# Decode attention with a SwiGLU block: two V rows per matmul, an identity held over twelve matmuls, one broadcast of the row maxima, and the last weight in three loads

## The chip, the cores and the metric

One core of a Trainium2 chip runs the kernel. The metric is the device time of one execution in microseconds (us), the median over several runs. "The changed kernel" is the kernel after the change; "before" is the one it was made from. A profile is one execution taken by the hardware profiler, and its times count from the start of the span. The profile counts 16 DMA engines for the core's loads; I call them queue engines. In the listings PE is the engine of the matmuls, PEld its loading of weights, DVE and ACT the engines of the elementwise work, and POOL an engine that is idle here after the first microseconds. A semaphore is a counter that engines wait for; PSUM is the memory that matmuls write to.

## The reference, cut to what matters

```python
# B=4 sequences, one new token each, D=640; 32 heads, 4096 cached keys, head size 192; F=1536
q = (layernorm(x) @ wq)                                  # per head: [192]
scores = einsum("bhqd,bhkd->bhqk", q, k_cache) * 192**-0.5
o = einsum("bhqk,bhkd->bhqd", softmax(scores), v_cache)
h = x + o.reshape(4, 1, 32*192) @ wo
out = h + (silu(ln(h) @ w_gate) * (ln(h) @ w_up)) @ w_down
```

K and V are 201 MB each in bf16 and every byte is used once. Everything else is small.

## The kernel before

The kernel goes through 64 steps. Step i treats two heads of one sequence: one K load and one V load of 3 MB each, into a ring of six buffers. A load is issued when the buffer's last reader is done.

```python
def tt(i, h):       # DVE: K times q, half a buffer at a time; 128 calls in all
    ... tensor_tensor(out=prod, in0=ring[K][half], in1=q broadcast, op=mult)

def red(i, h):      # PE: sum over the head size, 12 matmuls with the same identity as weights
    for j in range(J):
        ... e.matmul(psR[n % 3][:, 0:512], lhsT=identH, rhs=prod[..., j*R:(j+1)*R],
                     start=(j == 0), stop=(j == J - 1))

def max_b(i):       # PE: the two heads' maxima, each broadcast to 64 partitions
    for hh in range(2):
        ... e.matmul(psS[64*hh:64*hh+64, 128:129], lhsT=ones_row, rhs=negMc[0:1, hh:hh+1], ...)

def pv(i, ...):     # PE: 64 V rows per partition, one row per matmul, four column groups in turn
    for t in range(lo, hi):
        n = t % 4
        ... e.matmul(psO[p % 2][32*n:32*n+8, 0:192], lhsT=pbuf[b][:, t, :], rhs=v[:, t, :], ...)
```

After each group of four steps the sums are copied out of PSUM (`evac`), transposed by small fp32 matmuls (`o_t`), scaled (`o_tc`, giving `OT`) and multiplied by `wo`. At the end come the second layer norm (`lnT`), the gate and up products, their transpose `guT`, and 48 matmuls with `w_down`. The three last weights are loaded behind K and V into freed ring buffers:

```python
wg_land = dma("sp", ... wgsb, S_ring[...], [behind(n0)])
wu_land = dma("sp", ... wusb, S_ring[...], [behind(n0 + 1)])
wd_land = dma("sp", ... wdsb, S_ring[...], [behind(n0 + 2)])     # one load, 1920 KB
```

## Time and profile before

| | before |
|---|---|
| median of the first 3 runs | 1005.88 us (1005.46 to 1006.93) |
| instructions on PE (matmuls and weight loads) | 13472 |
| DMA in the loop | 425 to 435 GB/s by slice, mean 429, every slice full |
| instruction packets of 16 KB | 53 |
| last load: first and last of its 16 landings | 988.5 and 999.9 us |

The slices of the page before divide the span in 40. `DMA` is the busy share of the 16 queue engines in tenths.

```profile
PE   0676666666576576576576676676676676576585
DMA  9999999999999999999999999999999999999995
GB/s 394 426 435 430 426 431 427 428 431 427 429 429 427 429 429 431 428 427 431 427 430 428 430 426 431 425 433 430 425 431 429 428 429 428 431 428 429 428 425 248
```

DMA is full in every slice but the last, while PE has idle time throughout. So the loop is paced by the loads, at a mean of 429 GB/s, and computing less should not speed it up.

The page's DMA queues (packets, MB, share of the 16 engines' time) and its groups of instructions (line, engine, operation, shapes, count | busy us, mean ns | idle before, and what ended it):

```profile
q1 hardware_dynamic: 21472, 424.29, 98.9%
q8 instruction: 53, 0.87, 0.4%
...
L309 DVE TENSOR_TENSOR prod<-ring,qb 128x6144 f16<-128x6144 bf16 x128 | 429.2, 3354 | 308.3 <-DMA ring<-in_A_k_cache_dram 301.2
L319 PE MATMUL pb<-prod,identH 128*128 128x512 f16 x1536 | 470.6, 472 | 3.2 <-DVE prod L309 3.2
L319 PEld LDWEIGHTS pb<-prod,identH 128*128 128x128 f16 x1536 | 167.8, 116 | 262.1 <-issue 168.9
...
L381 PE MATMUL pb<-ring,pbuf 128*8 128x192 bf16 x4096 | 95.8, 246 | 0.2 <-ACT pbuf L356 0.2
L381 PEld LDWEIGHTS pb<-ring,pbuf 128*8 128x8 bf16 x4096 | 81.3, 87 | 3.7 <-issue 0.4
```

DVE waits 301 us for K. `q8 instruction`: the core also fetches its own program, here in 53 packets of 16384 bytes that take 1.07 us each in the mean.

The table of windows before (window, its length, then busy us and count of PE, PEld, DVE, ACT, POOL; granted clock as a share of PE's full clock, DMA share, GB/s):

```profile
300.00:305.00 5.00, 0.00 (x0) 0.00 (x0) 3.66 (x2) 0.00 (x0) 0.00 (x0) 0.76 1.00 428
985.00:990.00 5.00, 4.14 (x151) 3.42 (x146) 0.47 (x3) 3.15 (x8) 0.00 (x0) 1.00 0.87 371
990.00:995.00 5.00, 1.97 (x34) 0.84 (x26) 2.56 (x10) 1.58 (x2) 0.00 (x0) 0.70 0.55 231
995.00:1000.00 5.00, 2.15 (x28) 0.51 (x20) 1.40 (x2) 0.49 (x1) 0.00 (x0) 0.50 0.34 144
```

The last load was issued at 976.3, yet from 988 on only half of the queue engines, and later fewer, still work (DMA share 0.55 from 990, 0.34 from 995). The trace records 16 landings on the semaphore of each of these loads. I read them as one from each of the 16 queue engines. Sorted, for an early load and for the last one (wd), before:

```
a K load at the start   28.2 28.2 28.2 28.3 28.4 28.4 28.5 28.5 | 28.6 28.7 28.7 28.7 28.7 28.8 28.8 29.2
wd, the last load      988.5 988.7 988.8 988.9 989.2 990.1 991.9 993.0 | 998.1 998.4 998.4 999.0 999.3 999.6 999.7 999.9
```

Early, all 16 engines agree within 1.0 us. At the end eight are done by 993.0 and eight come at 998.1 to 999.9, so that first and last are 11.4 us apart. The distance grows evenly: in loads that begin to land at 162, 431, 698 and 966 us the last landing is 2.7, 5.3, 8.4 and 11.3 us behind the first. The kernel's wait for a load ends with the last landing, for wd at 999.9.

The tail of the timeline before (start, duration, instruction, count, idle before and what ended it):

```profile
995.39 1.77 PE L502 MATMUL pb<-wu_sb,lnT 128*4 128x384 bf16 x20
...
997.87 0.85 DVE L508 STREAM_TRANSPOSE guT<-gu 128x384 bf16<-128x384 bf16 x1
...
1000.05 1.77 PE L512 MATMUL pb<-wd_sb,guT 128*4 128x160 bf16 x48 [2.90 <-DMA wd_sb<-in_B_w_down_dram]
1001.87 0.32 DVE L515 CAST outsb<-pb 128x160 bf16<-128x160 f32 x1 [3.16 <-PE pb L512]
```

`guT` is ready at 998.7, but the matmuls with `w_down` wait for the last landing of wd at 999.9 and start at 1000.05.

### The profile page before, as it was taken

How to read it: one execution, taken by the hardware profiler on the slowest of the kernel's cores; microseconds unless marked ns; L12 is line 12 of the kernel's file. 1: busy time of each engine (PE TensorE's matmuls, PEld its weight loads, DVE VectorE, ACT ScalarE, POOL GpSimd, SP SyncE). 2: the span in 40 equal slices, each digit the busy share in tenths (PEclk: the TensorE clock that was granted, in tenths of full speed). 3: DMA queues.
4: the chain of work that ended last, by engine and by line, in shares of the span. 5: the costliest groups of instructions: out<-in, count | busy, mean ns of one | idle time of the engine just before them, and what ended most of it. 6: DMA issues, size and time to landing. Idle time of an engine off the chain costs nothing.

```text
span 1004.3 us, 14803 instructions
## 1 busy us (share of the span) xinstructions
PE 645.7 (64%) x6736; PEld 296.7 (30%) x6736; DVE 547.5 (55%) x450; ACT 119.7 (12%) x412; POOL 4.5 (0%) x19
## 2 busy tenths in 40 slices
PE   0676666666576576576576676676676676576585
PEld 0232232333232232232232232232332332232243
DVE  2546546546546546546546546546546546546562
ACT  0111011011011011011010110110111010111012
POOL 1000000000000000000000000000000000000000
PEclk9787887887887888887887887887887877877887
DMA  9999999999999999999999999999999999999995
GB/s 394 426 435 430 426 431 427 428 431 427 429 429 427 429 429 431 428 427 431 427 430 428 430 426 431 425 433 430 425 431 429 428 429 428 431 428 429 428 425 248
DMA packets 21582, 425.24 MB, mean 423 GB/s; under 512 B 2448, under 2 KB 2448, under 8 KB 4496
## 3 DMA queue, kind: packets, MB, share of 16 engines
q1 hardware_dynamic: 21472, 424.29, 98.9%
q8 instruction: 53, 0.87, 0.4%
q14 instruction: 9, 0.07, 0.0%
q10 hardware_dynamic: 48, 0.01, 0.0%
HBM read 424.29 MB, written 0.01 MB: 422 GB/s over the span
## 4 chain that ended last, share of the span: by engine, by line
DMA 68%; PE 21%; DVE 10%; SPq 1%; issue 0%; ACTq 0%; ACT 0%
DMA ring<-in_A_k_cache_dram 64%; PE pb L319 15%; DVE prod L309 7%; PE pb L381 3%; DMA wd_sb<-in_B_w_down_dram 2%; DMA xrow<-in_A_x_dram 2%; DVE sc L325 1%; PE pb L334 1%; SPq L294 1%; PE pb L276 1%; DVE msb L330 0%; PE pb L344 0%; PE pb L365 0%; PE pb L398 0%; SPq L300 0%
## 5 line engine op out<-in xcount | busy, mean ns | idle before, releaser
L309 DVE TENSOR_TENSOR prod<-ring,qb 128x6144 f16<-128x6144 bf16 x128 | 429.2, 3354 | 308.3 <-DMA ring<-in_A_k_cache_dram 301.2
L319 PE MATMUL pb<-prod,identH 128*128 128x512 f16 x1536 | 470.6, 472 | 3.2 <-DVE prod L309 3.2
L319 PEld LDWEIGHTS pb<-prod,identH 128*128 128x128 f16 x1536 | 167.8, 116 | 262.1 <-issue 168.9
L334 PE MATMUL pb<-identF,msb 128*1 128x128 f32 x128 | 34.7, 369 | 320.5 <-DVE msb L330 320.5
L325 DVE TENSOR_REDUCE sc<-pb 128x32 f32<-128x512 f32 x128 | 88.0, 688 | 111.8 <-PE pb L319 111.8
L334 PEld LDWEIGHTS pb<-identF,msb 128*1 128x1 f32 x128 | 5.5, 80 | 335.9 <-DVE msb L330 335.9
L349 ACT ACTIVATE negM<-pb 128x1 f32<-128x1 f32 x64 | 11.0, 171 | 721.0 <-PE pb L344 721.0
L381 PE MATMUL pb<-ring,pbuf 128*8 128x192 bf16 x4096 | 95.8, 246 | 0.2 <-ACT pbuf L356 0.2
L381 PEld LDWEIGHTS pb<-ring,pbuf 128*8 128x8 bf16 x4096 | 81.3, 87 | 3.7 <-issue 0.4
L356 ACT ACTIVATE pbuf<-sc,negM 64x64 bf16<-64x64 f32 x128 | 73.7, 576 | 3.1
L356 ACT ACTIVATION_READ_ACCUMULATOR pbuf<-sc,negM 64x1 f32 x128 | 41.6, 325 | 0.0
L371 ACT ACTIVATE qb<-pb 128x192 bf16<-128x192 f32 x64 | 21.1, 330 | 102.5 <-PE pb L365 102.5
L344 PEld LDWEIGHTS pb<-negMc,ones_row 1*64 1x64 f32 x256 | 12.8, 136 | 35.0 <-issue 33.4
L344 PE MATMUL pb<-negMc,ones_row 1*64 1x1 f32 x256 | 18.3, 206 | 0.7 <-DVE negMc L338 0.7
L365 PE MATMUL pb<-qsb,sel 4*64 4x192 bf16 x128 | 17.2, 265 | 1.0 <-ACT qsb L280 0.6
L338 DVE TENSOR_REDUCE negMc<-pb 1x2 f32<-1x128 f32 x64 | 17.4, 271 | 0.5 <-PE pb L334 0.5
L246 PE MATMUL pb<-mv,quadm 128*128 128x2 f32 x4 | 1.0, 312 | 23.4 <-DVE mv L244 23.4
L330 DVE TENSOR_REDUCE msb<-sc 128x1 f32<-128x64 f32 x64 | 14.1, 220 | 2.2
L365 PEld LDWEIGHTS pb<-qsb,sel 4*64 4x64 bf16 x128 | 6.7, 101 | 27.9 <-issue 26.3
L398 PE MATMUL pb<-r,orow 128*64 128x4 f32 x192 | 11.1, 233 | 0.4 <-ACT orow L387 0.4
L398 PEld LDWEIGHTS pb<-r,orow 128*64 128x64 f32 x192 | 9.7, 173 | 2.1 <-ACT orow L387 0.7
L242 DVE BATCH_NORM_STATS2 stats<-xrow 128x6 f32<-128x160 bf16 x1 | 0.3, 328 | 16.2 <-DMA xrow<-in_A_x_dram 16.2
(60 smaller groups left out, 71.8 us busy)
## 6 DMA issues: line engine op xcount, KB each, us to landing
ring<-in_A_k_cache_dram SPq DMA_DIRECT2D x64, 3072.0 KB, 30.4
ring<-in_A_v_cache_dram SPq DMA_DIRECT2D x63, 3072.0 KB, 23.4
wq_sb<-in_A_wq_dram SPq DMA_DIRECT2D x1, 7680.0 KB, 21.2
wo<-in_A_wo_dram SPq DMA_DIRECT2D x16, 480.0 KB, 23.8
ring<-in_A_v_cache_dram SPq DMA_DIRECT2D x2, 1536.0 KB, 19.7
wg_sb<-in_B_w_gate_dram SPq DMA_DIRECT2D x1, 1920.0 KB, 26.2
wu_sb<-in_B_w_up_dram SPq DMA_DIRECT2D x1, 1920.0 KB, 19.4
wd_sb<-in_B_w_down_dram SPq DMA_DIRECT2D x1, 1920.0 KB, 23.6
```

The source lines that it names most:

```text
L309: tk["tt", n] = op("dve", lambda e: e.tensor_tensor(out=prod[n % NPR][:, :, :], in0=ring[slot[c]][:, h * TH:(h + 1) * TH, :], in1=qbs[i % ...
L319: tk["red", n] = op("pe", lambda e, j=j: e.matmul(psR[n % 3][:, 0:TH * R], lhsT=identH[:, :], rhs=prod[n % NPR][:, :, j * R:(j + 1) * R], ...
L325: tk["rsum", n] = op("dve", lambda e: e.tensor_reduce(sc[i % 3][:, h * TH:(h + 1) * TH], psR[n % 3][:, 0:TH * R].rearrange("q (t r) -> q t ...
L330: tk["rmax", i] = op("dve", lambda e: e.tensor_reduce(msb[i % 2][:, 0:1], sc[i % 3][:, :], AX.X, ALU.max), [g("rsum", 2 * i), g("rsum", 2 ...
L334: tk["maxT", i] = op("pe", lambda e: e.matmul(psS[0:1, 0:128], lhsT=msb[i % 2][:, 0:1], rhs=identF[:, :], start=True, stop=True), [g("rmax ...
L338: tk["hmax", i] = op("dve", lambda e: e.tensor_reduce(negMc[i % 2][0:1, 0:2], psS[0:1, 0:128].rearrange("o (h q) -> o h q", h=2), AX.X, AL ...
L344: tk["maxB", i] = op("pe", lambda e, hh=hh: e.matmul(psS[64 * hh:64 * hh + 64, 128:129], lhsT=ones_row[0:1, :], rhs=negMc[i % 2][0:1, hh:h ...
L356: tk["exp", i] = op("act", lambda e, hh=hh, r=r: e.activation(out=pbuf[b][r, :, 2 * b + hh], in_=sc[i % 3][r, :], func=ACTF.Exp, bias=negM ...
L365: tk["qb", i] = op("pe", lambda e, hh=hh: e.matmul(psQ[64 * hh:64 * hh + 64, 0:DH], lhsT=sel[32 * n:32 * n + B, b, :], rhs=qsb[32 * n:32 * ...
L371: tk["qbc", i] = op("act", lambda e: e.activation(out=qbs[i % 2][:, :], in_=psQ[:, 0:DH], func=ACTF.Copy, scale=QS), [g("qb", i), g("tt", ...
L381: tk["pv", i] = op("pe", lambda e, t=t, n=n: e.matmul(psO[p % 2][32 * n:32 * n + 2 * B, 0:DH], lhsT=pbuf[b][:, t, :], rhs=v[:, t, :], star ...
L398: tk["oT", p] = op("pe", lambda e, j=j, hh=hh: e.matmul(psO[p % 2][64 * hh:64 * hh + 64, 256 + 4 * j:260 + 4 * j], lhsT=orow[p % 2][:, j:: ...
```

## The change

The intent is less work for PE, and a shorter wait for the last weight. PV takes two V rows per matmul: 16 columns of weights against 384 columns, of which only the two diagonal blocks are of use; the blocks that mix rows are left alone in PSUM. The identity is loaded for the first of 12 matmuls and kept for the other 11. The two maxima are broadcast by one matmul. wd comes in three loads.

```diff
+def held_matmul(e, out, lhsT, rhs, start, stop):
+    return e.add_instruction(mybir.InstMatmult(... ldweights=False, ...))
...
     def red(i, h):
-            tk["red", n] = op("pe", lambda e, j=j: e.matmul(
+            tk["red", n] = op("pe", lambda e, j=j: (e.matmul if j == 0 else partial(held_matmul, e))(
...
     def max_b(i):
-        for hh in range(2):
-            ... psS[64 * hh:64 * hh + 64, 128:129], lhsT=ones_row, rhs=negMc[i % 2][0:1, hh:hh + 1]
+        ... psS[:, 128:130], lhsT=ones_row, rhs=negMc[i % 2][0:1, 0:2]
...
     def pv(i, lo=0, hi=T):
-        for t in range(lo, hi):
-            n = t % 4
+        for t in range(lo, hi, 2):
+            n = (t // 2) % 4
-                psO[p % 2][32 * n:32 * n + 2 * B, 0:DH], lhsT=pbuf[b][:, t, :], rhs=v[:, t, :],
+                psO[p % 2][32 * n:32 * n + 4 * B, 0:2 * DH],
+                lhsT=pbuf[b][:, t:t + 2, :].rearrange("q t m -> q (t m)"),
+                rhs=v[:, t:t + 2, :].rearrange("q t d -> q (t d)"),
...
     def o_t(p):                     # sums the two diagonal blocks: twice the transposes
+                for k in range(2):
+                    ... lhsT=orow[p % 2][:, k * DH + j:(k + 1) * DH:3], start=(k == 0), stop=(k == 1)
...
-    wd_land = dma("sp", ... wdsb, S_ring[(n0 + 2) % NS], [behind(n0 + 2)])
+    WDC = [(0, 6, sem("s_wd0")), (6, 10, sem("s_wd1")), (10, CF, sem("s_wd2"))]
+    for lo, hi, k in WDC:
+        t = dma("sp", ... wdsb[:, lo:hi, :], k, [behind(n0 + 2)])     # 960, 640 and 320 KB
```

More of the change, by code (lines that the diff above doesn't have):

```diff
@@ L1 @@
 import math
+from functools import partial
 import concourse.bass as bass
@@ L91, in emit @@
         block.sync(run("sp"))
+def held_matmul(e, out, lhsT, rhs, start, stop):
+    return e.add_instruction(mybir.InstMatmult(
+        name=e.bass.get_next_instruction_name(), engine=mybir.EngineType.PE, start_tensor_calc=start,
+        stop_tensor_calc=stop, tile_size=(128, 128), tile_position=(0, 0), ldweights=False,
+        ins=[e.lower_ap(rhs), e.lower_ap(lhsT, for_matmul_weights=True)], outs=[e.lower_ap(out)]))
 class ExitGuard:
@@ L118, in build_kernel @@
     NS, NPR = 6, 3
+    OC = 2 * DH
     QS = 2.0 ** -4
@@ L145, in build_kernel @@
     r32 = sb("r32", [128, 32], FP32)
-    ones_row = sb("ones_row", [1, 64], FP32)
+    ones_row = sb("ones_row", [1, 128], FP32)
     epsv = sb("epsv", [128, 1], FP32)
@@ L155, in build_kernel @@
     negMc = [sb(f"negMc{j}", [1, 2], FP32) for j in range(2)]
-    negM = [sb(f"negM{j}", [128, 1], FP32) for j in range(2)]
+    negM = [sb(f"negM{j}", [128, 2], FP32) for j in range(2)]
     lsb = [sb(f"lsb{j}", [128, B], FP32) for j in range(2)]
     invL = sb("invL", [128, B], FP32)
-    orow = [sb(f"orow{j}", [128, DH], FP32) for j in range(2)]
+    orow = [sb(f"orow{j}", [128, 2 * DH], FP32) for j in range(2)]
     OT = [sb(f"OT{j}", [128, 3, B], BF16) for j in range(2)]
@@ L342, in max_b @@
     def max_b(i):
-        for hh in range(2):
-            tk["maxB", i] = op("pe", lambda e, hh=hh: e.matmul(
-                psS[64 * hh:64 * hh + 64, 128:129], lhsT=ones_row[0:1, :], rhs=negMc[i % 2][0:1, hh:hh + 1],
-                start=True, stop=True), [g("hmax", i), pool_done])
+        tk["maxB", i] = op("pe", lambda e: e.matmul(
+            psS[:, 128:130], lhsT=ones_row[0:1, :], rhs=negMc[i % 2][0:1, 0:2],
+            start=True, stop=True), [g("hmax", i), pool_done])
     def neg_m(i):
-        tk["negM", i] = op("act", lambda e: e.activation(out=negM[i % 2][:, :], in_=psS[:, 128:129], func=ACTF.Copy,
+        tk["negM", i] = op("act", lambda e: e.activation(out=negM[i % 2][:, :], in_=psS[:, 128:130], func=ACTF.Copy,
                                                          scale=alpha), [g("maxB", i)])
@@ L356, in exps @@
             tk["exp", i] = op("act", lambda e, hh=hh, r=r: e.activation(
-                out=pbuf[b][r, :, 2 * b + hh], in_=sc[i % 3][r, :], func=ACTF.Exp, bias=negM[i % 2][r, 0:1],
+                out=pbuf[b][r, :, 2 * b + hh], in_=sc[i % 3][r, :], func=ACTF.Exp, bias=negM[i % 2][r, hh:hh + 1],
                 scale=alpha, accum_out=lsb[p % 2][r, b:b + 1]),
@@ L377, in pv @@
         v = ring[slot[c]]
-        for t in range(lo, hi):
-            n = t % 4
+        for t in range(lo, hi, 2):
+            n = (t // 2) % 4
             land = landed[c][min(t // TH, len(landed[c]) - 1)]
             tk["pv", i] = op("pe", lambda e, t=t, n=n: e.matmul(
-                psO[p % 2][32 * n:32 * n + 2 * B, 0:DH], lhsT=pbuf[b][:, t, :], rhs=v[:, t, :],
-                start=(b == 0 and t < 4), stop=(b == B - 1 and t >= T - 4)), [land, g("exp", i), g("otc", p - 2)])
+                psO[p % 2][32 * n:32 * n + 4 * B, 0:2 * DH],
+                lhsT=pbuf[b][:, t:t + 2, :].rearrange("q t m -> q (t m)"),
+                rhs=v[:, t:t + 2, :].rearrange("q t d -> q (t d)"),
+                start=(b == 0 and t < 8), stop=(b == B - 1 and t >= T - 8)), [land, g("exp", i), g("otc", p - 2)])
         released[c] = tk["pv", i]
     def evac(p):
-        tk["evac", p] = op("act", lambda e: e.activation(out=orow[p % 2][:, :], in_=psO[p % 2][:, 0:DH],
+        tk["evac", p] = op("act", lambda e: e.activation(out=orow[p % 2][:, :], in_=psO[p % 2][:, 0:2 * DH],
                                                          func=ACTF.Copy), [g("pv", B * p + B - 1), g("oT", p - 2)])
@@ L397, in o_t @@
             for hh in range(2):
-                tk["oT", p] = op("pe", lambda e, j=j, hh=hh: e.matmul(
-                    psO[p % 2][64 * hh:64 * hh + 64, 256 + 4 * j:260 + 4 * j], lhsT=orow[p % 2][:, j::3],
-                    rhs=r32[:, hh:2 * B:2], start=True, stop=True), [g("evac", p), pool_done])
+                for k in range(2):
+                    tk["oT", p] = op("pe", lambda e, j=j, hh=hh, k=k: e.matmul(
+                        psO[p % 2][64 * hh:64 * hh + 64, OC + B * j:OC + B * (j + 1)],
+                        lhsT=orow[p % 2][:, k * DH + j:(k + 1) * DH:3],
+                        rhs=r32[:, 2 * B * k + hh:2 * B * (k + 1):2], start=(k == 0), stop=(k == 1)),
+                        [g("evac", p), pool_done])
     def inv_l(p):
@@ L406, in o_tc @@
         tk["otc", p] = op("dve", lambda e: e.tensor_tensor(
-            out=OT[p % 2][:, :, :], in0=psO[p % 2][:, 256:256 + 3 * B].rearrange("q (j b) -> q j b", b=B),
+            out=OT[p % 2][:, :, :], in0=psO[p % 2][:, OC:OC + 3 * B].rearrange("q (j b) -> q j b", b=B),
             in1=invL[:, None, :].broadcast_to([128, 3, B]), op=ALU.mult),
@@ L490, in build_kernel @@
                   S_ring[(n0 + 1) % NS], [behind(n0 + 1)])
-    wd_land = dma("sp", lambda e: e.dma_start(wdsb[:, :, :].rearrange("q c n -> q (c n)"),
-                                              wd[:, :].rearrange("(q c) n -> q (c n)", c=CF)),
-                  S_ring[(n0 + 2) % NS], [behind(n0 + 2)])
+    WDC = [(0, 6, sem("s_wd0")), (6, 10, sem("s_wd1")), (10, CF, sem("s_wd2"))]
+    wd_land = {}
+    for lo, hi, k in WDC:
+        t = dma("sp", lambda e, lo=lo, hi=hi: e.dma_start(
+            wdsb[:, lo:hi, :], wd[:, :].rearrange("(q c) n -> q c n", c=CF)[:, lo:hi, :]), k, [behind(n0 + 2)])
+        for c in range(lo, hi):
+            wd_land[c] = t
     zg = op("dve", lambda e: e.memset(PB[0][:, 0:FQ], 0.0), [g("red", 2 * NP - 1)])
@@ L513, in build_kernel @@
                 psH[32 * n:32 * n + B, 0:DQ], lhsT=guT[:, c, 0:B], rhs=wdsb[:, c, n * DQ:(n + 1) * DQ],
-                start=False, stop=(c == CF - 1), skip_group_check=True), [gut, wd_land, ln2])
+                start=False, stop=(c == CF - 1), skip_group_check=True), [gut, wd_land[c], ln2])
     a = op("dve", lambda e: e.tensor_copy(out=outsb[:, :], in_=psH[:, 0:DQ]), [a])
```

## The prediction

> **What bounds the kernel.** The loads. The page's 40 slices show DMA 9 in every slice but the last, at 425 to 431 GB/s; 424.3 MB over the span is 422 GB/s.[...] PE is busy 64% and DVE 55%; the 64% of the chain of waits put on K loads says the same. In the loop all the work removed from PE is off the critical path: DVE waits 301 us for K loads, and the ring is always filled ahead (K landing takes 30 us after issue).
>
> **What the change does on PE.** 5376 instructions fewer of 13472: PV 4096 pairs become 2048 (-4096), the 128x128 identity is loaded 128 times, not 1536 (-1408), max broadcast -256, output transposes +384. PV time hardly falls: 64 pairs take 1.49 us (23 ns each[...]), and 32 of twice the columns should take 1.3 to 1.6 us. The identity loads are hidden: 12 matmuls take 2.76 us at full clock (230 ns each), perhaps 2.6 after; at half clock 427 ns each, unchanged. So in the loop: zero.
>
> **Where it can count: the tail.** In the table of windows DMA falls to 371 GB/s at 985-990, 231 at 990-995 and 144 at 995-1000, though every load was issued by 976.3. The semaphore records show why: the 16 increments of one load come within 1.0 us at 28 us, but the last load's run from 988.5 to 999.9; eight of them, 988.5 to 993.0, and eight, 998.1 to 999.9. Half of the queue engines lag, and the lag grows evenly. The instruction queue moves 53 packets of 16 KB, about 1.07 us each, durations repeating with period 8: instruction fetch in turn over eight engines.[...] 53/8 = 6.6 fetches per engine against about 9 us of lag is 1.2 to 1.45 us each (estimate). 5376 fewer instructions are 21 fewer fetches: 32, 4 per engine, so the late engines gain 2.6 fetches, estimate 3.2 to 3.7 us, at every late landing: K62 (962.4), V63, wu (995.3), wd (999.9).
>
> **After the last landing.** Before: wd lands 999.9, 48 matmuls 1.77 us, cast at 1001.87. guT was ready at about 998.7, so 40 of the 48 matmuls can now run before the last piece: about 1.3 us, less if guT becomes the limit. Against it: the chain after PV gets 12 more transpose instructions (12 took 0.70 us; +0.6) and a wider evacuation (128x384 took 0.49, 128x192 0.33; +0.16). The last compute chain starts from K62's landing, so it moves with it. By estimate gate and up matmuls end near 994.4, guT 995.9, wd's last piece 996.4, matmuls 997.7: 4.1 us earlier.
>
> **Predicted** 1002.0 us, 8 in 10 within 1000.6 to 1004.2. Faster by over 2%: 0.01; within 2%: 0.98; slower: 0.01.
>
> **What shows it right or wrong.** Loop DMA still 427 to 431 GB/s; about 32 instruction packets; the last load's late increments some 3.5 us earlier, the early ones unmoved; PE busy and weight-load counts down without time; the last PE group of wd short after the last piece. Idle of DVE for K unchanged.
>
> **What would make it wrong.** Lag not from fetches (other engine differences): then only about 0.5 to 1 us. A colder PE clock in the last 25 us (12 matmuls 5.1 instead of 2.76 us) would delay guT and eat the gain.[...]

The sum: wd's last piece at 996.4 and the end of the matmuls at 997.7 are 4.1 us earlier than before, and 1006.1 less 4.1 is 1002.0. Its 21 fetches fewer follow from the trace: 53 packets for 13472 instructions are 254 for each, and 5376 over 254 is 21. Its 1.3 to 1.6 us for PV rest on the measured 1.49 us, for the same number of columns in all.

## The result, and the profile after

| | before | changed |
|---|---|---|
| median of 4 runs each, same rounds | 1006.11 us | 1001.66 us (1001.34 to 1002.74) |
| instructions on PE | 13472 | 8096 |
| instruction packets of 16 KB | 53 | 32 |
| last landing of wd | 999.9 us | 995.5 us |

The changed kernel is 4.45 us faster by these medians. The ratio is 0.9957, with a 95% interval of 0.994 to 0.9975; it is clear of noise. Ratios here are the mean time of one kernel's fast runs over that of the other's fast runs of the same rounds, so not quite the ratio of the quoted medians.

The page after, the same parts:

```profile
PE   0676676676676676676677686676676666676686
DMA  9999999999999999999999999999999999999996
GB/s 393 427 438 426 427 435 428 426 434 427 427 431 431 425 429 433 430 427 427 433 428 428 432 428 428 427 434 427 428 431 433 425 428 432 428 428 430 431 423 287
...
q1 hardware_dynamic: 21760, 424.29, 99.2%
q8 instruction: 32, 0.52, 0.2%
...
L319 DVE TENSOR_TENSOR prod<-ring,qb 128x6144 f16<-128x6144 bf16 x128 | 429.1, 3353 | 303.6 <-DMA ring<-in_A_k_cache_dram 295.9
L97 PE MATMUL pb<-prod,identH 128*128 128x512 f16 x1408 | 434.2, 472 | 0.0
...
L391 PE MATMUL pb<-ring,pbuf 128*16 128x384 bf16 x2048 | 94.7, 326 | 0.2 <-ACT pbuf L365 0.2
```

The loop is as it was: full DMA, and DVE waits 296 us for K where it waited 301. PV is busy 94.7 us after and 95.8 before, with half the matmuls at twice the width. PE's matmul time as a whole did not fall: 661.4 us against 645.7. What fell is the number of instructions, and with it the instruction packets: 53 to 32.

The windows after, and the landings of the last piece of wd:

```profile
300.00:305.00 5.00, 1.51 (x5) 0.19 (x3) 4.96 (x4) 0.00 (x0) 0.00 (x0) 0.88 1.05 446
985.00:990.00 5.00, 2.41 (x38) 1.90 (x38) 2.10 (x10) 0.83 (x3) 0.00 (x0) 0.64 0.91 377
990.00:995.00 5.00, 3.37 (x40) 1.22 (x40) 1.38 (x4) 1.50 (x2) 0.00 (x0) 0.50 0.51 209
995.00:1000.00 5.00, 1.77 (x48) 1.43 (x48) 1.09 (x2) 0.00 (x0) 0.00 (x0) 0.50 0.02 5
```

```
wd's last piece        988.9 989.0 989.1 989.3 989.5 990.3 991.8 993.5 | 993.6 995.3 995.3 995.3 995.4 995.4 995.4 995.5
```

The early half lands when it did before; the late half comes 4 us sooner. The 995 to 1000 window is now almost empty of loads.

```profile
985.32 1.25 PE L412 MATMUL pb<-r,orow 128*64 128x4 f32 x24 [0.59 <-ACT orow L399]
...
992.39 1.82 PE L522 MATMUL pb<-wu_sb,lnT 128*4 128x384 bf16 x20
...
994.92 0.85 DVE L528 STREAM_TRANSPOSE guT<-gu 128x384 bf16<-128x384 bf16 x1
...
995.82 1.77 PE L532 MATMUL pb<-wd_sb,guT 128*4 128x160 bf16 x48 [1.62 <-DVE guT L528]
997.64 0.33 DVE L535 CAST outsb<-pb 128x160 bf16<-128x160 f32 x1 [1.88 <-PE pb L532]
```

The final cast starts at 997.64 instead of 1001.87. The matmuls with `w_down` now wait for `guT` (995.8) and not for a load (995.5): the two ends arrive almost together.

### The profile page after: what moved, and what is told of

Read it like the earlier page. It is cut to its first block, busy times and chain, and to the rows that moved or that the text cites. A ratio compares the mean times of both kernels' runs of the same rounds, so it can differ in the third digit from the quotient of the medians.

```text
span 1000.1 us, 9429 instructions
## 1 busy us (share of the span) xinstructions
PE 661.4 (66%) x4752; PEld 122.6 (12%) x3344; DVE 547.6 (55%) x450; ACT 122.6 (12%) x412; POOL 4.5 (0%) x19
## 4 chain that ended last, share of the span: by engine, by line
DMA 65%; PE 23%; DVE 10%; SPq 1%; issue 1%; ACT 0%; ACTq 0%; DVEq 0%
DMA ring<-in_A_k_cache_dram 63%; PE pb L97 13%; DVE prod L319 8%; PE pb L391 3%; DMA xrow<-in_A_x_dram 2%; PE pb L329 2%; DVE sc L335 1%; PE pb L344 1%; PE pb L412 1%; PE pb L353 1%; SPq L304 1%; PE pb L286 1%; DVE msb L340 1%; PE pb L374 0%; PE pb L522 0%
## 5 line engine op out<-in xcount | busy, mean ns | idle before, releaser
L97 PE MATMUL pb<-prod,identH 128*128 128x512 f16 x1408 | 434.2, 472 | 0.0
L358 ACT ACTIVATE negM<-pb 128x2 f32<-128x2 f32 x64 | 11.0, 172 | 713.5 <-PE pb L353 713.5
L391 PE MATMUL pb<-ring,pbuf 128*16 128x384 bf16 x2048 | 94.7, 326 | 0.2 <-ACT pbuf L365 0.2
L329 PE MATMUL pb<-prod,identH 128*128 128x512 f16 x128 | 61.3, 479 | 3.2 <-DVE prod L319 3.2
L353 PEld LDWEIGHTS pb<-negMc,ones_row 1*128 1x128 f32 x128 | 19.3, 189 | 280.5 <-issue 258.1
L391 PEld LDWEIGHTS pb<-ring,pbuf 128*16 128x16 bf16 x2048 | 46.4, 89 | 27.5 <-issue 0.5
L353 PE MATMUL pb<-negMc,ones_row 1*128 1x2 f32 x128 | 24.8, 261 | 0.7 <-DVE negMc L348 0.7
L412 PE MATMUL pb<-r,orow 128*64 128x4 f32 x384 | 20.0, 231 | 0.6 <-ACT orow L399 0.6
L412 PEld LDWEIGHTS pb<-r,orow 128*64 128x64 f32 x384 | 18.6, 174 | 2.4 <-ACT orow L399 1.0
L329 PEld LDWEIGHTS pb<-prod,identH 128*128 128x128 f16 x128 | 12.7, 99 | 32.7 <-issue 28.3
```

The costliest lines, as they stand in the source:

```text
L97: return e.add_instruction(mybir.InstMatmult(name=e.bass.get_next_instruction_name(), engine=mybir.EngineType.PE, start_tensor_calc=start, ...
L329: tk["red", n] = op("pe", lambda e, j=j: (e.matmul if j == 0 else partial(held_matmul, e))(psR[n % 3][:, 0:TH * R], lhsT=identH[:, :], rhs ...
L353: tk["maxB", i] = op("pe", lambda e: e.matmul(psS[:, 128:130], lhsT=ones_row[0:1, :], rhs=negMc[i % 2][0:1, 0:2], start=True, stop=True), ...
L391: tk["pv", i] = op("pe", lambda e, t=t, n=n: e.matmul(psO[p % 2][32 * n:32 * n + 4 * B, 0:2 * DH], lhsT=pbuf[b][:, t:t + 2, :].rearrange(" ...
L412: tk["oT", p] = op("pe", lambda e, j=j, hh=hh, k=k: e.matmul(psO[p % 2][64 * hh:64 * hh + 64, OC + B * j:OC + B * (j + 1)], lhsT=orow[p % ...
```

## The experiments

The theory is that each instruction packet holds up the queue engine that carries it, that half of the engines carry all of PE's, and that the last of the 16 sets every landing. So the gain is the number of packets saved. Rivals: the gain comes from PE having less to do or reading fewer weights; or it comes from the split of wd. Each experiment had five rounds against before on the same chip, unless it says otherwise.

### a: the changed kernel with wd in one load

```diff
-    WDC = [(0, 6, ...), (6, 10, ...), (10, CF, ...)]   # three loads
+    wd_land = dma("sp", ... wdsb, S_ring[(n0 + 2) % NS], [behind(n0 + 2)])
```

> The changed kernel with wd again in one load. Theory (instruction fetch makes half of the queue engines late; fewer fetches give the gain; the split of wd is idle because guT, ready at 995.8 us in the profile of the changed kernel, comes after wd's last piece at 995.5): within 0.5 us of the changed kernel, 1001.7 us, wd landing at about 995.5. Rival (the split gave about 1.3 us of the gain, as the prediction's paragraph on the last landing had it): 1003.0 us.

Measured: 1001.49 us, ratio to before 0.9952 (0.9939 to 0.9964). wd landed at 995.5, and `guT` was ready at 996.8. The split gives nothing that these runs resolve in the changed kernel, so the gain is from elsewhere. (In this profile `guT` came 1.0 us later than in that of the changed kernel, and the 48 matmuls took 1.00 us instead of 1.77; why was not looked into.)

### b: the kernel before with only wd in three loads

> The kernel before with only wd in three loads. There guT is ready at 998.7 us and wd lands at 999.9, so 40 of the 48 matmuls can run ahead: theory 1.0 to 1.3 us faster than before, about 1004.9 us. Rival (the split is worth nothing anywhere): 1006.1 us.

Measured: 1006.56 us against 1006.68, ratio 1.0001 (0.9989 to 1.0014). A miss: the expected gain of 1.0 to 1.3 us did not show. In the profile of this run the last piece landed at 1001.1, 1.2 us later than in the profile of before, and the 48 matmuls ran from 1000.24 to 1002.0, where with one load they could have started only at the landing, 1001.1, and ended some 0.9 us later. So the split did its work in that profile, but the landing moves by as much from run to run. The interval still allows up to 1.1 us; what it excludes is that the split made the 4.45 us.

### c: the changed kernel with 5376 idle instructions on POOL

```diff
+    def filler(i):      # called in each step: 168 waits on a semaphore that is already up, counted as 84 instructions
+        op("pool", lambda e: [e.wait_ge(S_x, 64) for _ in range(168)] and None, [tk["tt", 2 * i]])
```

> The changed kernel with 5376 instructions added on the idle POOL engine: waits on a semaphore that is already up, 84 behind each K multiply, moving no data. Nothing on PE, DVE or the loads changes. Theory (fetch): the instruction queue shows about 53 packets of 16 KB instead of 32, the late half of the queue engines is again some 4 us later (last wd piece 999.5 to 1000), and the time goes back to 1005 to 1006 us. If POOL's fetches go to other queue engines than PE's, other engines become late and the loss is smaller. Rival (the gain came from PE doing less): stays at 1001.7 us.

Measured: 1022.47 us, ratio 1.0159 (1.0145 to 1.0173). The queues of this run:

```profile
q8 instruction: 32, 0.52, 0.2%
q14 instruction: 52, 0.42, 0.1%
```

I count two waits as one instruction: in run d, 10752 instructions counted so came in 84 packets of 8192 bytes, 64 bytes each, and PE's 256 in 16384 bytes (table below) are 64 bytes each too. The fillers were fetched not on PE's queue but on another (9 packets there in the changed kernel), and in packets of 8 KB. The builder also merged the pacing waits, so that POOL ran its fillers in one go from 512 us: the 8 KB packets then come about every 11.5 us, from 519 us on. The landings, sorted:

```
520 us    520.0 520.0 520.0 520.5 521.0 521.0 521.4 521.8 522.6 523.1 523.1 523.2 523.2 523.4 523.4 523.4
838 us    838.2 838.2 838.4 838.5 838.6 838.6 838.7 838.8 838.8 838.8 838.9 839.2 839.2 839.4 840.4 853.5
the last  1003.5 1003.5 1003.7 1003.7 1003.7 1003.7 1003.8 1003.8 1003.9 1003.9 1003.9 1003.9 1004.0 1004.2 1005.5 1017.0
```

Exactly one queue engine falls behind, from the time when POOL's fetches start. With 43 small packets (0.35 MB of 425) it ends 11.5 us behind the next one, and it holds up the others too: they are at 1003.5 to 1005.5 instead of 989 to 995.5, since the kernel reloads a ring buffer only behind readers that waited for its last landing. PE, DVE and the loads are those of the changed kernel. The direction is the theory's. The size is not what was expected (1005 to 1006), because all packets went to one engine: one landing, 1017.0, is late, and not eight.

### d: the same with 10752

> The same with 10752 instructions added on POOL. Theory (fetch): 74 packets, twice the loss of the run with 5376, so 1009 to 1010 us, linear in the number of packets. Rival (PE work): stays at 1001.7 us.

Measured: 1474.48 us (four runs). This run does not test what it should. POOL started its 10752 fillers at 512 us and simply ran on alone until 1471.6 us, 89 ns for each (with 93 packets on q14 against 9 in the changed kernel, an 8 KB packet has 128 of them, 11.4 us, near the 11.5 between packets in run c); its own instructions ended last. Of use is only that wd's last landing, 1018.8, is near that of run c: until then POOL had fetched at the same rate.

### e: the kernel before with only the held identity

```diff
-            ... e.matmul(psR[n % 3][:, 0:TH * R], lhsT=identH, ...)
+            ... (e.matmul if j == 0 else partial(held_matmul, e))(psR[n % 3][:, 0:TH * R], lhsT=identH, ...)
```

> The kernel before with only the identity held over 12 matmuls: 1408 weight loads fewer, nothing else. Theory (fetch): 5 or 6 packets fewer (47 or 48), at 0.21 us a packet (4.4 us of later landing over 21 packets, before against changed), so the last load's last increment about 998.8 and the time about 1.2 us below before, 1005.1. Rival (PE time or hidden weight loads count): PE's loop is off the critical path, so 1006.3, unchanged.

Measured: 1005.05 us against 1006.43, ratio 0.9983 (0.9971 to 0.9996). Its page has

```profile
PE 645.8 (64%) x6736; PEld 141.1 (14%) x5328; DVE 547.5 (55%) x450; ACT 119.7 (12%) x412; POOL 4.5 (0%) x19
...
q8 instruction: 47, 0.77, 0.3%
```

47 packets and a last landing of 998.9, as the theory had it. PE's matmul time is the same to 0.1 us (645.8 and 645.7): the weight loads taken out had been hidden behind matmuls, and still the kernel is faster, by 0.4 to 2.9 us by the interval.

### f: the kernel before with only the two V rows per matmul

> The kernel before with only the two V rows per matmul (with its wider evacuation and its 384 more transpose instructions): 3712 instructions fewer. Theory (fetch): 14 or 15 packets fewer (38 or 39), last landing about 996.9, time about 3.1 us below before, 1003.2. Rival (all the gain is in the other parts): 1006.3 or, with the longer chain of transposes, 1007.

Measured: 1003.89 us against 1006.43, ratio 0.9972 (0.9959 to 0.9986), with 38 packets and a last landing of 997.7. The gain is 2.5 us where 3.1 was expected, inside the interval.

### g: the changed kernel with 5376 small instructions back on PE

```diff
+    def filler():       # called once per step, before the transpose of the row maxima
+        for _ in range(42):
+            op("pe", lambda e: e.matmul(psS[0:4, 300:301], lhsT=identB[:, 0:4], rhs=identB[:, 0:1], start=True, stop=True), [kidb])
```

> The changed kernel with 42 tiny matmuls and their weight loads per pair (5376 instructions, one column wide, into an unused column), placed where PE sits idle for the row maxima. PE keeps the changed kernel's wide PV matmuls, held identity and one broadcast. Theory (fetch): 53 packets again on the same queue as before, eight late queue engines, last landing 999.5 to 1000, time 1005.5 to 1006. Rival (the shapes of the matmuls or the fewer reads of weights made the gain, not the count): 1001.7 to 1002.5, since the fillers fit in idle time.

Measured: 1007.09 us, ratio to before 1.0002 (0.9989 to 1.0015).

```profile
PE 719.9 (72%) x7440; PEld 196.0 (19%) x6032; DVE 547.6 (54%) x450; ACT 122.5 (12%) x412; POOL 4.5 (0%) x19
...
q8 instruction: 53, 0.87, 0.4%
...
1001.58 0.85 DVE L534 STREAM_TRANSPOSE guT<-gu 128x384 bf16<-128x384 bf16 x1
...
1002.48 1.00 PE L538 MATMUL pb<-wd_sb,guT 128*4 128x160 bf16 x48 [1.61 <-DVE guT L534]
```

With the instruction count of before, and all of the changed kernel's wide matmuls, held weights and single broadcast, there are 53 packets again, the landings end at 1000.7, and the gain is gone. By the median it is 1 us slower than expected (the five runs spread from 1005.5 to 1007.82, and two lie within the expectation). In the profile, which is the slowest of the five, `guT` comes at 1002.4, 1.7 us after the last landing, so here the compute chain at the end is what finishes last. That the fillers themselves lengthened it is likely, but was only argued.

Together, e, f, g and the two kernels give this table. "Late half" is the mean of the last eight of the last load's 16 landings, in the profile of each; "blocks" divides PE's instructions by 256, which fits the counts (253 to 257 instructions for each packet in the six rows). The medians come from two series: before measured 1006.11 beside the changed kernel, and 1006.43 beside e to h.

| | PE instructions | blocks | packets | late half, us | median, us |
|---|---|---|---|---|---|
| before | 13472 | 52.6 | 53 | 999.1 | 1006.11 |
| g: changed, with PE fillers | 13472 | 52.6 | 53 | 999.3 | 1007.09 |
| e: held identity only | 12064 | 47.1 | 47 | 998.2 | 1005.05 |
| f: two V rows only | 9760 | 38.1 | 38 | 996.5 | 1003.89 |
| changed | 8096 | 31.6 | 32 | 995.1 | 1001.66 |
| h: changed, 640 fewer | 7456 | 29.1 | 29 | 995.0 | 1000.82 |

From before to changed the late half comes 4.0 us sooner over 21 packets, 0.19 us for each packet. If they are shared by eight engines, each packet costs its engine eight times that, about 1.5 us (an estimate), while the trace shows a packet taking 1.07 us.

The landings of single loads confirm this. In the changed kernel a PE packet starts at 302 us. The two loads around it, each landing counted from the load's first one:

```
297 us   0.0 0.2 0.2 0.4 0.5 0.6 0.8 1.5 1.6 1.8 1.8 1.8 1.9 1.9 2.0 2.1
304 us   0.0 0.2 0.2 0.4 0.5 0.6 0.8 1.5 1.6 1.8 1.8 1.8 1.9 1.9 2.1 3.5
```

One landing has moved by 1.5 us and the other fifteen have stayed. Compared load by load, 30 of the 32 packets of the changed kernel and 50 of the 53 of before show as such a step, with a median of 1.55 and 1.53 us. The packets at 302, 557 and 809 us, eight apart in order, each set the last landing anew (2.1 to 3.5, 3.6 to 5.0, 5.1 to 6.5 us after the first), and the seven between them bring seven other landings up to about the same level, so the fetches take eight engines in turn. The few 8 KB packets of the other instruction queue move other landings, by about 0.7 us each (0.67, 0.68 and 0.71 at 134, 598 and 822 us in the changed kernel); this is why the early half is not quite even either.

The last landing is thus that of the engine with most fetches. Counted in turn, over the packets fetched before wd has landed, it carries 7, 7, 6, 5, 4 and 4 in the order of the table.

### h: 640 instructions fewer still

```diff
-    orow = [sb(f"orow{j}", [128, 2 * DH], FP32) ...]       # o_t in fp32: 24 matmul records for 12 calls
+    orow = [sb(f"orow{j}", [128, 2 * DH], BF16) ...]       # 12 for 12; r32 likewise as a bf16 copy
-    msb, negMc, ones_row in FP32;  max_t with identF
+    msb, negMc, ones_row in BF16;  max_t with identB       # the maximum only shifts the exponent
+    the two memsets of the gate and up banks before o_tc instead of behind it
```

> The changed kernel with the output transposes and the row-max transpose and broadcast in bf16 (one pass on PE instead of two: 640 instructions fewer) and the two clears of the gate and up banks moved ahead of the last OT. Theory: 2 or 3 packets fewer (29 or 30), landings 0.5 us earlier; the chain after the last PV 0.6 us shorter from 12 instead of 24 transpose instructions and 0.2 to 0.4 us from the rest; 1.0 to 1.4 us faster than the changed kernel, 1000.3 to 1000.7 us. Rival (the load's end alone sets the time): 0.5 us faster.

Measured: 1000.82 us, ratio to before 0.9943 (0.993 to 0.9955), correct against the reference, 29 packets. The two passes show in the traces as matmul records: the last `o_t` has 24 of them for its 12 calls in the changed kernel (1.25 us), 12 here (0.44 us). Now `guT` is ready at 994.8, before wd's last piece at 996.1. The expected landings 0.5 us earlier did not come: the last one is 0.6 us later than in the changed kernel, and the late half is at 995.0 against 995.1. By the count in turn, 29 packets leave four on the fullest engine, as 32 do. So the gain is from the shorter chain of computation; how much of it each of its parts gives was not separated.

### i: on which queue engines is the late half?

> The changed kernel with three small loads of 2, 4 and 8 rows queued behind wd, each with its own semaphore, to see on which queue engines the late half sits.[...] if it is every second one, half and half. No theory of mine says which. Time: within 1 us of 1001.7.

Measured, one run: 1002.74 us (before: 1005.72). The loads of 2, 4 and 8 rows show one early record (975.8, 976.2, 976.5; its size is not recorded) and then 2, 4 and 8 landings, as many as they have rows:

```
2 rows  989.2 992.3
4 rows  989.4 990.0 992.5 993.8
8 rows  989.2 989.6 990.2 990.2 992.7 994.0 995.5 995.8
```

Two or three of the eight landings of the largest come as late as wd's late half (995.5, 995.8 and perhaps 994.0), the others in the time of the early half (989.2 to 992.7). So the landings of this one load fall in both halves. Which queue engines they are was not shown, since the trace does not name an engine; the three cases in the expectation rested on an order of the engines that no run here shows, so the third (every second engine, half of the landings late) can't be judged. Which engines carry PE's fetches stays open. That they are eight in turn is seen in the steps above, and it fits the durations of the packets, which repeat with a period of eight (1099, 1099, 1087, 1018, 1018, 1074, 1078, 1060 ns, and again).

### j, k, l: the faster version again, and the split of wd where it should count

j is the changed kernel, k is run h's kernel, and l is that kernel with wd in one load, all in the same rounds.

> The changed kernel itself again, so that the two kernels below are compared with it in the same rounds: 1001.7 us, 0.995 to 0.996 of before.

> The kernel with 640 instructions fewer (run h) again, in the same rounds as the changed kernel. From the first runs 0.8 us faster than the changed kernel, 1000.8 us; if it was luck, equal.

> Run h with wd in one load. In run h guT is ready at 994.8 us and wd's last piece lands at 996.1, so here the split should matter, unlike in the changed kernel: all 48 matmuls (1.8 us) come after the landing, 1.0 to 1.2 us slower than run h, 1001.9 us. If the split is worth nothing here too: 1000.8 us.

Measured: j 1002.01 us, ratio 0.9956 (0.9943 to 0.9968); k 1001.13, ratio 0.9948 (0.9935 to 0.996); l 1002.08, ratio 0.9957 (0.9943 to 0.9971). The version with 640 instructions fewer is 0.9 us faster than the changed kernel here, and 0.84 by the medians of the first runs of each, which were not in the same rounds; the intervals overlap, but both series say the same, so it is the fastest version found, by a little. The end of the timeline of k, then of l:

```profile
994.10 0.85 DVE L530 STREAM_TRANSPOSE guT<-gu 128x384 bf16<-128x384 bf16 x1
...
995.01 1.77 PE L534 MATMUL pb<-wd_sb,guT 128*4 128x160 bf16 x48 [1.62 <-DVE guT L530]
996.83 0.32 DVE L537 CAST outsb<-pb 128x160 bf16<-128x160 f32 x1 [1.88 <-PE pb L534]
```

```profile
993.27 0.85 DVE L526 STREAM_TRANSPOSE guT<-gu 128x384 bf16<-128x384 bf16 x1
...
996.00 1.77 PE L530 MATMUL pb<-wd_sb,guT 128*4 128x160 bf16 x48 [3.44 <-DMA wd_sb<-in_B_w_down_dram]
997.83 0.33 DVE L533 CAST outsb<-pb 128x160 bf16<-128x160 f32 x1 [3.71 <-PE pb L530]
```

In l the matmuls wait for the one load until 996.0, although `guT` was there at 994.1; in k they start at once and the last pieces land meanwhile. The split is worth 1.0 us in the profiles and 0.95 by the medians. It pays only where the compute chain arrives before the load, and that holds in k but not in the changed kernel.

## Why the prediction was right or wrong

It said 1002.0 us, within 1000.6 to 1004.2, and measured was 1001.66. Its gain of 4.1 us stands against 4.45.

- **The loads bound the kernel; PE's savings in the loop are worth zero.** Right. The slices of DMA are full after as before, and DVE's wait for K is 296 us against 301. In run e PE's matmul time is unchanged, in run g it is higher, and the time follows the packets in both.
- **Instruction fetch makes half of the queue engines late.** Right. The packets in the trace are of 16384 bytes, and PE's instructions over 256 give 52.6, 47.1, 38.1, 31.6 and 29.1 for 53, 47, 38, 32 and 29 packets. The predicted 32 packets were counted.
- **Late landings 3.2 to 3.7 us sooner.** Right in mechanism, too small: wd's last landing moved by 4.4 us. The term that was mis-sized is mainly the number of fetches saved: the prediction took the mean of the late engines, 2.6, but the last landing is that of the engine with most, which goes from 7 to 4. The cost of one fetch, 1.2 to 1.45 us in the prediction, is 1.5 by the steps. Three times 1.5 is 4.5 us (an estimate).
- **The split of wd: about 1.3 us, "less if guT becomes the limit".** `guT` became the limit, and run a shows no share of the split. The prediction's own sum already ended with `guT` at 995.9 plus 1.8 us of matmuls. It measured 995.8; the part that gave in was the last piece, 995.5 instead of 996.4. So the two errors, landings too late and a split worth something, hardly touched the total; that it fits to 0.34 us is partly luck.
- **The chain after PV: +0.6 for the transposes, +0.16 for the copy.** Right: 0.70 us for 12 became 1.25 for 24, and 0.33 became 0.49. That this chain moves with K62 was right too: DVE started on K62 at 958.54 instead of 962.45.
- **12 matmuls with the held identity, "perhaps 2.6" us at full clock.** A guess for which the record gives no numbers. Wrong, and without effect: before they took 2.76 us, after 2.77 (976.32 to 979.09 in the trace of the changed kernel), both at a granted clock of 1.00.
- **"PE busy and weight-load counts down".** Half wrong: the count of weight loads went from 6736 to 3344, but the busy time of matmuls rose from 645.7 to 661.4 us.
- **A colder clock at the end** did not come in the mean of the span: 0.826 before, 0.831 after. In the windows above the clock did fall sooner after (0.64 against 1.00 at 985 to 990, 0.50 against 0.70 at 990 to 995), but little hung on it: the 48 matmuls took 1.77 us in both, and two short groups before them 0.2 us more each (the 12 with `wo` 0.57 against 0.38).

## What to carry to other kernels

This kernel is bound by its loads, and its program was fetched over the same queue engines: each packet of 16 KB put the engine that carried it back by about 1.5 us, and each load was as late as its last engine (wd at 999.9 us with 53 packets, 995.5 with 32). In a kernel where the profile shows the same, count instructions as well as bytes. Removing instructions that cost an engine no time at all (1408 hidden weight loads in run e) still saved 0.4 to 2.9 us, and putting 5376 instructions on an idle engine cost 16 us over before (run c). Splitting the last load paid 1.0 us where its consumer was ready before it landed (k against l), and nothing that was resolved where it was not (run a), so look at which of the two waits ended last, and look again after every other change.
